# Loading and multiplying the first query projection chunk by chunk for all eight heads

## The chip, the cores and the metric

One core of one Trainium2 chip. The metric is the device time of one execution in microseconds, as a median over runs. The profiles are each of one execution; a profile's span is some 1.8 us shorter than the time of its run.

## The reference

Two independent attention blocks, A and B, whose outputs are concatenated. Each has its own x, cached K and V, and weights, all in bf16:

```python
B, Sq, D = 16, 32, 1024
Hq, Hkv, Sk, Dh = 32, 4, 512, 128
q = (x @ wq).reshape(B, Sq, Hq, Dh).transpose(0, 2, 1, 3)
scores = jnp.einsum("bhqd,bhkd->bhqk", q, k) * (Dh ** -0.5)
p = softmax(scores)
o = jnp.einsum("bhqk,bhkd->bhqd", p, v)
out = o.transpose(0, 2, 1, 3).reshape(B, Sq, Hq * Dh) @ wo
# ... the same for B; the two are concatenated on the last axis
```

What matters is the very first product: x @ wq for the first eight of A's 32 query heads. Nothing else can start before it. The sum over D = 1024 runs in eight chunks of 128.

## The kernel before

The start of the program loads x and the first eight heads' weights, multiplies them as they arrive, and only then enters the long loop over scores, values and projections. `load_w0(d0, d1, h0, h1, eng)` loads chunks d0 to d1 of the weights for heads h0 to h1, on SP's queue unless another engine is named. `load_x_transposed` loads two chunks of x through a transposing load. NF is 6, REP is 8, HC is 4, DC is 8, TT is 4.

```python
load_x(TT // 2, TT, nc.scalar)
# ...
load_x(0, TT // 2)
load_w0(0, 1, 0, NF // 2)              # chunk 0, heads 0..2   96 KB  SP
load_w0(0, 1, NF // 2, NF, nc.scalar)  # chunk 0, heads 3..5   96 KB  ACT
load_w0(1, 2, 0, NF)                   # chunk 1, heads 0..5  192 KB  SP
load_w0(2, 3, 0, NF, nc.scalar)        # chunk 2, heads 0..5  192 KB  ACT
load_x_transposed(2)
load_w0(3, 4, 0, NF)                   # chunk 3, heads 0..5  192 KB  SP
load_w0(0, HC, NF, REP)                # chunks 0..3, heads 6 and 7, rows of 512 bytes
load_w0(HC, HC + 1, 0, REP)            # chunk 4, all heads
# ... chunks 5 to 7 and the rest of x, then the loads of the main loop
warm_up(22)                            # matmuls on a constant, meant to raise the clock
for k, ts in enumerate(((0, TT // 2), (TT // 2, TT))):
    transpose_x(0, *ts, nc.vector.tensor_copy)
    transpose_x(1, *ts, nc.scalar.copy, spare[k])
for ts in ((0, TT // 2), (TT // 2, TT)):
    first_heads(range(0, NF // 2), (0,), *ts)   # chunk 0, heads 0..2, in two halves
first_heads(range(NF // 2, NF), (0,))           # chunk 0, heads 3..5
first_heads(range(NF), (1, 2, 3))               # chunks 1..3, heads 0..5
first_q += [...]                                # accumulators of heads 6 and 7
first_heads(range(NF, REP), range(HC))          # heads 6 and 7, chunks 0..3
first_heads(range(REP), range(HC, DC - 1))      # chunks 4..6, all heads
# ... chunk 7, then the copies out of PSUM; the main loop follows
```

Of the kernel before, what the change touches and what calls it, by code (L numbers as in the profile page):

```python
# [9 lines left out]
FP32 = mybir.dt.float32  # L10
# [6 lines left out]
P = 128  # L17
# [3 lines left out]
REP = HQ // HKV  # L21
# [160 lines left out]
def kernel(  # L182
# [14 lines left out]
    nc = tc.nc  # L197
# [3 lines left out]
    DC = D // P  # L201
# [3 lines left out]
    NW = 512  # L205
# [12 lines left out]
    def fast_path(ok_i):  # L218
        with ExitStack() as fctx:
# [6 lines left out]
            psum = enter(tc.tile_pool(name="psum", bufs=2, space=bass.MemoryType.PSUM))  # L226
# [190 lines left out]
            ob = {}  # L417
# [37 lines left out]
            NF = REP - 2  # L455
            HC = DC // 2
# [10 lines left out]
            def load_x_transposed(d0):  # L467
                nc.sync.dma_start_transpose(
                    out=xT[0][:, d0:d0 + 2, :],
                    in_=A_x.flatten_outer_dims()[:, d0 * P:(d0 + 2) * P],  # L470
                )

            def load_w0(d0, d1, h0, h1, eng=nc.sync):
                eng.dma_start(  # L474
                    out=w0[d0 // HC][:, d0 % HC:(d1 - 1) % HC + 1, h0 * DH:h1 * DH],
                    in_=wq_v[:, d0:d1, h0 * DH:h1 * DH],
                )
# [2 lines left out]
            nc.scalar.preload_act_table_set("natural_log_exp_and_others")  # L480
            load_x(0, TT // 2)
            load_w0(0, 1, 0, NF // 2)
            load_w0(0, 1, NF // 2, NF, nc.scalar)
            load_w0(1, 2, 0, NF)
            load_w0(2, 3, 0, NF, nc.scalar)
            load_x_transposed(2)
            load_w0(3, 4, 0, NF)
            load_w0(0, HC, NF, REP)
            load_w0(HC, HC + 1, 0, REP)
            load_x_transposed(HC)  # L490
            load_w0(HC + 1, DC - 1, 0, REP)
            load_x_transposed(HC + 2)
            load_w0(DC - 1, DC, 0, REP)
            load_wq(0, 2, 0, 2)
# [9 lines left out]
            first_q = []  # L504
# [12 lines left out]
            def transpose_x(d, t0, t1, copy, ps=None):  # L517
                if ps is None:
                    ps = psum.tile([P, NTOK], BF16, name="xT_ps", tag="ob")
                for tt in range(t0, t1):  # L520
                    nc.tensor.transpose(
                        ps[:, tt * P:(tt + 1) * P], x_sb[:, tt, d * P:(d + 1) * P], ident[:]
                    )
                ts = slice(t0 * P, t1 * P)
                copy(out=xT[0][:, d, ts], in_=ps[:, ts])

            def first_heads(heads, dcs, t0=0, t1=TT):
                ts = slice(t0 * P, t1 * P)
                for dc in dcs:
                    for h in heads:  # L530
                        nc.tensor.matmul(  # L531
                            first_q[h][:, ts],
                            lhsT=w0[dc // HC][:, dc % HC, h * DH:(h + 1) * DH],
                            rhs=xT[0][:, dc, ts],
                            start=(dc == 0 and t0 == 0),
                            stop=(dc == DC - 1),
                        )

            warm_up(22)
            for k, ts in enumerate(((0, TT // 2), (TT // 2, TT))):  # L540
                transpose_x(0, *ts, nc.vector.tensor_copy)
                transpose_x(1, *ts, nc.scalar.copy, spare[k])
            for ts in ((0, TT // 2), (TT // 2, TT)):
                first_heads(range(0, NF // 2), (0,), *ts)
            first_heads(range(NF // 2, NF), (0,))
            first_heads(range(NF), (1, 2, 3))
            first_q += [psum.tile([P, NW], FP32, name="q_ps", tag="ob")[:] for _ in range(2)]
            first_heads(range(NF, REP), range(HC))
            first_heads(range(REP), range(HC, DC - 1))
            for n, h in enumerate((0, 2, 4, 6, 5, 7, 1, 3)):  # L550
                first_heads((h,), (DC - 1,))
                copy = nc.vector.tensor_copy if n % 2 else nc.scalar.copy
# [115 lines left out]
    ok_i = flag.tile([1, 1], I32, name="ok_i")  # L668
    total = 2 * 2 * NG * QW
    ok = fast_path(ok_i)  # L670
    with tc.If(ok < total, preferred_fallthrough_block=True, label="general"):
        general_path(tc, problems, out_flat)
# [30 lines left out]
```

## Time and profile before

| | before |
|---|---|
| time, median of 3 runs | 343.0 us (342.91 to 343.46) |
| span of the profiled run | 341.1 us |
| TensorE busy | 98% of the span |
| chunk 1 lands / chunk 1's matmuls start | 6.23 / 6.28 us |
| first projection ends | 18.97 us |

The prediction below shows the chain and the waits. To these belongs the list of DMA issues from the start of the program (stretch 1.2 to 2.0 us). Its columns: tiles, the queue that issued, how often, size, and the time from issue to landing.

```profile
w_sb<-in_A_wq_dram SPq DMA_DIRECT2D x1, 192.0 KB, 4.5
w_sb<-in_A_wq_dram ACTq DMA_DIRECT2D x1, 192.0 KB, 4.7
x_sb<-in_A_x_dram ACTq DMA_DIRECT2D x1, 128.0 KB, 3.0
w_sb<-in_A_wq_dram SPq DMA_DIRECT2D x1, 96.0 KB, 2.8
w_sb<-in_A_wq_dram ACTq DMA_DIRECT2D x1, 96.0 KB, 3.0
```

The first two lines are chunk 1 (SP) and chunk 2 (ACT).

### The profile page before, as it was taken

What the parts mean: (1) busy time and instruction counts of PE and PEld (TensorE: products, weight loads), DVE (VectorE), ACT (ScalarE), POOL (GpSimd) and SP (SyncE); (2) the same over time, 40 slices, a digit from 0 to 9 for tenths busy, and PEclk for the clock granted to TensorE, in tenths of its full rate; (3) what the DMA queues carried; (4) which work ended last, traced back from release to release, by engine and by line L of the source; (5) the groups of instructions that cost most, each with busy time, mean ns of one, the idle gap of its engine ahead of it and who ended that gap; (6) DMA issues with size and microseconds to landing.
All of it is one profiled execution on the core that took longest, in us unless ns stands there. A gap on an engine that the chain in (4) does not pass through costs nothing.

```text
span 341.1 us, 5436 instructions
## 1 busy us (share of the span) xinstructions
PE 334.5 (98%) x2074; PEld 212.8 (62%) x2113; DVE 265.4 (78%) x335; ACT 185.3 (54%) x208; POOL 47.0 (14%) x206
## 2 busy tenths in 40 slices
PE   8999999999999999999999999999999999999996
PEld 5455666666666666666666666666666666666555
DVE  0047988888988898888888988879888888889540
ACT  2057666666667667666645545555554555555110
POOL 0001110011111111110012221222122101111100
PEclk9999999999999999999999999999999999999999
DMA  7999999999996998899999955998449995430001
GB/s 199 298 188 274 288 250 225 205 254 250 301 258 144 241 222 232 197 294 308 322 293 290 240 125 147 338 284 222 118 106 307 357 194 152 115 93 9 17 19 33
DMA packets 128622, 71.70 MB, mean 210 GB/s; under 512 B 76880, under 2 KB 127824, under 8 KB 128592
## 3 DMA queue, kind: packets, MB, share of 16 engines
q1 hardware_dynamic: 127504, 69.78, 82.5%
q0 software_dynamic: 384, 1.05, 0.8%
q10 hardware_dynamic: 704, 0.49, 0.5%
q8 instruction: 17, 0.28, 0.3%
q14 instruction: 13, 0.11, 0.1%
HBM read 50.59 MB, written 2.10 MB: 154 GB/s over the span
## 4 chain that ended last, share of the span: by engine, by line
PE 96%; DMA 2%; issue 1%; ACT 0%; SPq 0%; ACTq 0%
PE f_ps L320 31%; PE q_ps L301 28%; PE ob L425 17%; PE s_ps L357 16%; PE q_ps L531 4%; DMA w_sb<-in_A_wq_dram 1%; DMA out_dram<-o_sb 0%; ACT o_sb L329 0%; SPq L465 0%; SPq L474 0%; ACTq L329 0%; ACT p_sb L365 0%; ACTq L365 0%
## 5 line engine op out<-in xcount | busy, mean ns | idle before, releaser
L365 ACT ACTIVATE p_sb<-s_ps,shift 128x1024 bf16<-128x1024 f32 x128 | 142.7, 1115 | 97.5 <-PE s_ps L357 86.3
L376 DVE TRANSPOSE_TENSOR_REDUCE parts<-p_sb 128x32 f32<-128x1024 bf16 x128 | 158.7, 1240 | 20.8 <-ACT p_sb L365 19.3
L320 PE MATMUL f_ps<-wo_sb,oT 128*128 128x512 bf16 (+1 forms) x524 | 127.6, 366 | 0.6
L301 PE MATMUL q_ps<-xT,wq_sb 128*128 128x512 bf16 x430 | 113.0, 379 | 0.6
L425 PE MATMUL ob<-p_sb,v_sb 128*128 128x256 bf16 x512 | 76.8, 273 | 0.8
L357 PE MATMUL s_ps<-qT,kT 128*128 128x256 bf16 x512 | 76.8, 273 | 0.0
L320 PEld LDWEIGHTS <-oT 128*128 128x128 bf16 x544 | 53.2, 98 | 35.3
L357 PEld LDWEIGHTS <-kT 128*128 128x128 bf16 x512 | 56.9, 113 | 28.3
L301 PEld LDWEIGHTS <-wq_sb 128*128 128x128 bf16 x448 | 43.8, 98 | 32.2
L425 PEld LDWEIGHTS <-v_sb 128*128 128x128 bf16 x512 | 50.1, 98 | 20.0
L447 DVE TENSOR_TENSOR oT<-r,ob 128x512 bf16<-128x512 f32 x64 | 43.9, 686 | 19.8 <-PE ob L425 19.4
L411 DVE STREAM_TRANSPOSE r<-rall 128x512 f32<-128x512 f32 x64 | 44.2, 691 | 1.1
L309 ACT CAST qT<-q_ps 128x512 bf16<-128x512 f32 x56 | 32.7, 583 | 16.5 <-PE q_ps L301 16.5
L394 POOL COPY half<-cs 64x32 f32<-64x32 f32 x32 | 6.6, 206 | 231.5 <-DVE cs L384 231.4
L329 ACT CAST o_sb<-f_ps 128x512 bf16<-128x512 f32 (+1 forms) x17 | 9.5, 559 | 23.6 <-PE f_ps L320 23.6
L531 PE MATMUL q_ps<-xT,w_sb 128*128 128x512 bf16 (+1 forms) x66 | 14.1, 369 | 0.6 <-DMA w_sb<-in_A_wq_dram 0.6
L406 DVE RECIPROCAL rall<-sums 128x32 f32<-128x32 f32 x32 | 10.4, 326 | 3.3 <-POOL sums L403 3.3
L384 DVE TENSOR_REDUCE cs<-parts 128x32 f32<-128x128 f32 x32 | 12.1, 377 | 1.1
L553 DVE CAST qT<-q_ps 128x512 bf16<-128x512 f32 x4 | 2.5, 683 | 13.2 <-PE q_ps L531 13.2
L531 PEld LDWEIGHTS <-w_sb 128*128 128x128 bf16 x67 | 6.4, 97 | 8.0 <-DMA w_sb<-in_A_wq_dram 1.1
L553 ACT CAST qT<-q_ps 128x512 bf16<-128x512 f32 x4 | 2.1, 599 | 12.8 <-PE q_ps L531 12.8
L331 POOL DMA_DIRECT2D out_dram<-o_sb x8 | 4.6, 575 | 29.2 <-ACT o_sb L329 29.2
(25 smaller groups left out, 48.1 us busy)
## 6 DMA issues: line engine op xcount, KB each, us to landing
v_sb<-in_A_v_cache_dram SPq DMA_DIRECT2D x16, 512.0 KB, 5.4
wq_sb<-in_B_wq_dram SPq DMA_DIRECT2D x8, 1024.0 KB, 6.0
wo_sb<-in_A_wo_dram SPq DMA_DIRECT2D x8, 1024.0 KB, 7.5
v_sb<-in_B_v_cache_dram SPq DMA_DIRECT2D x16, 512.0 KB, 4.6
wo_sb<-in_B_wo_dram SPq DMA_DIRECT2D x8, 1024.0 KB, 8.5
wq_sb<-in_A_wq_dram SPq DMA_DIRECT2D x5, 1024.0 KB, 6.7
wq_sb<-in_A_wq_dram SPq DMA_DIRECT2D x2, 512.0 KB, 7.3
kT<-in_A_k_cache_dram SPq DMA_TRANSPOSE x64, 4.4
```

Source lines behind the costliest of these rows:

```text
L301: nc.tensor.matmul(ps[:], lhsT=w[:, dc, (h % 4) * DH:(h % 4 + 1) * DH], rhs=xT[pr][:, dc, :], start=(dc == 0), stop=(dc == DC - 1),)
L309: nc.scalar.copy(out=qT[pr, g][:, :, hl, :], in_=ps[:].rearrange("p (b s) -> p b s", s=SQ),)
L320: nc.tensor.matmul(ps[:, 0:width], lhsT=oT[pr, tt][:, h, :], rhs=wo_tiles[pr, nh, h // REP][:, h % REP, off:off + width], start=(h == 0), ...
L357: nc.tensor.matmul(s_ps[:, c, :], lhsT=kT[:, i % GRP, c, :], rhs=qT[pr, g][:, b, :, :].rearrange("p h s -> p (h s)"), start=True, stop=True,)
L365: nc.scalar.activation(out=p_sb[:], in_=s_ps[:], func=ACTF.Exp, bias=shift[:], scale=SCALE)
L376: nc.vector.tensor_reduce(out=parts[k][:, q, :, :].rearrange("p c h -> p (c h)"), in_=st[i]["p"][:].rearrange("p c (h s) -> p (c h) s", s=SQ),
L384: nc.vector.tensor_reduce(out=cs[:], in_=parts.pop(k)[:].rearrange("p q c h -> p q h c"), axis=AX.X, op=ALU.add,)
L406: nc.vector.reciprocal(out=rall[:, k, :], in_=quad.pop(k)[:])
L411: nc.vector.transpose(out=r[:].rearrange("p n s -> p (n s)"), in_=rall[:, k, o * 2 * REP:(o + 1) * 2 * REP] .unsqueeze(2).to_broadcast([P, ...
L425: nc.tensor.matmul(ob[j][:, q, :], lhsT=v_sb[:, i % GRP, c, :], rhs=st[i]["p"][:, c, :], start=(c == 0), stop=(c == KC - 1),)
L447: nc.vector.tensor_tensor(out=out, in0=rcp.pop(j)[:].rearrange("p (q h) s -> p q h s", h=REP), in1=ob.pop(j)[:].rearrange("p q (h s) -> p ...
L531: nc.tensor.matmul(first_q[h][:, ts], lhsT=w0[dc // HC][:, dc % HC, h * DH:(h + 1) * DH], rhs=xT[0][:, dc, ts], start=(dc == 0 and t0 == 0 ...
```

## The change

The intent: load each chunk in one piece for all eight heads, in rows of 2 KB, alternating between the two queues at first. Heads 6 and 7 then join from chunk 0 on instead of following after chunk 3, and the 512-byte rows go.

```diff
-            load_w0(0, 1, NF // 2, NF, nc.scalar)
-            load_w0(1, 2, 0, NF)
-            load_w0(2, 3, 0, NF, nc.scalar)
+            load_w0(0, 1, NF // 2, REP, nc.scalar)
+            load_w0(1, 2, 0, REP)
+            load_w0(2, 3, 0, REP, nc.scalar)
             load_x_transposed(2)
-            load_w0(3, 4, 0, NF)
-            load_w0(0, HC, NF, REP)
+            load_w0(3, 4, 0, REP)
             load_w0(HC, HC + 1, 0, REP)
             load_x_transposed(HC)
-            load_w0(HC + 1, DC - 1, 0, REP)
+            for d in range(HC + 1, DC - 1):
+                load_w0(d, d + 1, 0, REP)
@@
+            first_q += [psum.tile([P, NW], FP32, name="q_ps", tag="ob")[:] for _ in range(2)]
             for ts in ((0, TT // 2), (TT // 2, TT)):
                 first_heads(range(0, NF // 2), (0,), *ts)
-            first_heads(range(NF // 2, NF), (0,))
-            first_heads(range(NF), (1, 2, 3))
-            first_q += [psum.tile([P, NW], FP32, name="q_ps", tag="ob")[:] for _ in range(2)]
-            first_heads(range(NF, REP), range(HC))
-            first_heads(range(REP), range(HC, DC - 1))
+            first_heads(range(NF // 2, REP), (0,))
+            first_heads(range(REP), range(1, DC - 1))
```

## The prediction

> **What bounds the kernel now.** I read the page from the top: busy shares, then the slices, then the chain of work that ended last, and from there only the first 24 us, because the change touches nothing later.
>
> The page's busy line, slices and chain:
>
> ```profile
> span 341.1 us, 5436 instructions
> ...
> PE 334.5 (98%) x2074; PEld 212.8 (62%) x2113; DVE 265.4 (78%) x335; ACT 185.3 (54%) x208; POOL 47.0 (14%) x206
> ...
> PE   8999999999999999999999999999999999999996
> ...
> PEclk9999999999999999999999999999999999999999
> ...
> PE 96%; DMA 2%; issue 1%; ACT 0%; SPq 0%; ACTq 0%
> ```
>
> TensorE is busy in every slice at the full granted clock, and 96% of the chain is matmuls. A matmul that is saved, or a wait that is added, anywhere on it moves the end by its own length. DMA has 2% of the chain, which is where the change acts. The chain in order of time over the first 24 us (start, length, what) shows it:
>
> ```profile
> 1.26 0.44 SPq L474
> 1.70 0.05 issue
> 1.75 4.48 DMA w_sb<-in_A_wq_dram
> 6.23 0.05 issue
> 6.28 2.33 PE q_ps L531 x10
> 8.61 0.05 issue
> 8.66 10.31 PE q_ps L531 x47
> 18.97 0.43 PE q_ps L301 x2
> ```
>
> The end of the program hangs on one load: the second load that SP issues for w_sb, which is chunk 1 of the weights (six heads, 192 KB). It is issued at about 1.7 us, lands at 6.23, and from 6.28 TensorE runs without a wait: 57 recorded matmuls (58 in the program, one record is missing) until 18.97, then straight into the rest. So 12.69 us for 58, or 0.2188 us each. The waits of TensorE, asked over the whole program, are only two:
>
> ```profile
> PE q_ps L513 <- PEq L687: 0.9, 1, 0.9
> PE q_ps L531 <- DMA w_sb<-in_A_wq_dram: 0.6, 1, 0.6
> ```
>
> The first is the program's start. The second is the wait that this change can move: TensorE has finished chunk 0 and sits 0.6 us until chunk 1 lands. The same spot in the timeline of TensorE (start, length, group):
>
> ```profile
> 3.40 0.88 PE L521 MATMUL xT_ps<-ident,x_sb 128*128 128x128 bf16 x8
> 4.17 1.50 PE L531 MATMUL q_ps<-xT,w_sb 128*128 128x256 bf16 x9
> 6.28 12.69 PE L531 MATMUL q_ps<-xT,w_sb 128*128 128x512 bf16 x57 [0.59 <-DMA w_sb<-in_A_wq_dram]
> ```
>
> The nine matmuls from 4.17 to 5.67 are chunk 0: three heads in two halves each, then three whole ones. How fast the loads go while this wait is set, and later when only 2-KB rows move, the DMA view tells (stretches 3.2 to 6.3 and 10.45 to 11.6 us):
>
> ```profile
> DMA packets 1201, 0.72 MB, mean 232 GB/s; under 512 B 747, under 2 KB 1201, under 8 KB 1201
> q1 hardware_dynamic: 906, 0.42, 71.7%
> q10 hardware_dynamic: 295, 0.30, 31.9%
> ...
> DMA packets 290, 0.39 MB, mean 339 GB/s; under 512 B 112, under 2 KB 112, under 8 KB 290
> ```
>
> In the first stretch both queues (q1 is SP's, q10 ACT's) share the engines, rows are 768 or 1,536 bytes, and pieces of 256 bytes of a transpose come in: 232 GB/s. In the second, SP alone moves 2-KB rows: 339 GB/s.
>
> **What the Trainium skill says.** "DMA: Bandwidth & Descriptors", section "Queues, rings and completion order": each DMA engine takes turns between the queues it has work for, a packet at a time. The trace agrees: both queues have data in the same stretch (0.42 and 0.30 MB). So bytes that are added to ACT's queue delay SP's chunk 1 too. The same page, section "Issuing engines are not separate DMA queues", says that loads from several engines run on the same 16 DMA engines and interleave; so the two queues are no second source of bandwidth. "Perfetto Trace Analysis", section "DMA Optimizations", says that transfers under 2 KB carry a significant overhead each; 339 against 232 GB/s is in line with it, although the slower stretch also holds the transpose, so rows are not its only difference. "TensorE: Matmul & The Clock Gate", part 1, says that the clock halves after an idle window of about 3.4 us; the trace has 0.59 us of idle here and the granted clock stays 1.00, so it doesn't contradict it.
>
> **The change part by part.** The count and shape of matmuls stay the same: 67 in this stage (6 halves and 61 whole). Bytes stay the same: 2 MB of weights, 1 MB of x apart from the 256 KB read twice. SP issues ten loads of this stage after its x in both kernels, ACT two.
>
> 1. Moved to before the wait: heads 6 and 7 of chunk 0. Chunk 0 becomes 6 halves and 5 whole matmuls, and 56 instead of 58 come after the wait: 2 x 0.2188 = 0.44 us less after it. Before the wait, chunk 0 ends at 5.67 + 0.44 = 6.11 instead of 5.67. That alone would eat most of the 0.59 us of idle time, for free: a gain of 0.44 us if chunk 1 landed when it does now.
>
> 2. But chunk 1 lands later. Its load grows from 192 to 256 KB, and the part of chunk 0 on ACT's queue, which shares the engines with it, from 96 to 160 KB. SP's own part of chunk 0 (96 KB) and the x loads are as before; chunk 2's extra 64 KB on ACT's queue lies mostly behind. So 128 KB more pass before chunk 1 is complete. At 232 GB/s that is 131,072 B / 232 = 0.56 us; at the 339 of 2-KB rows 0.39 us. I take 0.48. The wait then ends at 6.28 + 0.48 = 6.76 (between 6.67 and 6.84).
>
> 3. The part on ACT's queue: now "96 KB, 3.0 us" from issue at 1.34, so it lands at 4.34. With 64 KB more, at half of 232 GB/s as the queues share, up to 0.56 us later, 4.9. Head 3 needs it at 4.17 + 6 half matmuls of 0.11 = 4.83. A stall of 0.1 us is possible, but chunk 0 then ends at 6.2, still before 6.76: it costs nothing.
>
> 4. Later chunks. Chunk 2 needs its weights and its transposed x at 6.76 + 8 x 0.2188 = 8.51. The transpose is issued at 2.22 and takes 5.2 us now, so 7.42; 192 KB more lie ahead of it or beside it (64 each in chunk 0, 1 and 2): 0.58 to 0.85 us, so 8.0 to 8.3. It holds, by 0.2 to 0.5 us; this is the narrow place. Chunk 3 (192 KB now lands at 3.7 + 4.5 = 8.2) has 256 KB more before its end, so about 9.2, and is needed at 10.26. Chunk 4 has the same bytes ahead of it as now, with the 512-byte rows of heads 6 and 7 gone, lands at 9.8 or earlier and is needed at 12.0. Everything after lands as now or a little earlier and has 1 us or more of slack.
>
> 5. After 18.97 nothing changes: the same instructions in the same order on every engine, and TensorE has no wait left there that an earlier load could shorten.
>
> Sum: +0.48 us for the later landing, -0.44 us for two matmuls that go before it, so +0.04 us (between -0.05 and +0.12). On 343.0 that is 343.0 to 343.1. **I predict 343.1 us.** The gain in load efficiency of the 2-KB rows comes in a stage in which, after chunk 1, TensorE is the slower side.
>
> **Rivals.**
> - Chunk 1 lands hardly later (about 6.4), because 2-KB rows move faster and the 256-byte transpose pieces start later and disturb less. For it: 339 against 232 GB/s. Against: on-chip queues share a packet at a time, so ACT's extra bytes still count. It would make 342.7.
> - The slowest DMA engine sets the landing. The mean rate says chunk 1 should be in by about 5.5, yet it lands at 6.23: some engines run well behind the others. If their lag grows with the bytes (192 to 256 KB, so 4/3 of the roughly 2.3 us that it now takes to move), the wait ends at about 7.0: 343.3.
> - The wait moves on to chunk 2, if the transposed x lands after its slack of 0.2 to 0.5 us: 0.2 to 0.5 us more, 343.3 to 343.6. The slow transpose pieces speak for it; against it, whatever delays the transpose delays chunk 1 as well, and both slide together.
> - The longer idle time lowers the clock: with under 1 us of idle time the trace gives no reason, and it would make about 344.7 if half of a window of 3.4 us were lost.
>
> **Range and chances.** The worked-out spread of the wait's end, 6.4 to 7.3, gives -0.3 to +0.6 us; runs of the kernel before spread from 342.91 to 343.46. So 342.5 to 343.8 for eight in ten. Two per cent is 6.9 us; the whole stage before the first wait's end is 6.3 us and cannot be lost or gained by this. Faster by over 2%: 0.005; within 2%: 0.985; slower by over 2%: 0.01.
>
> **What would show it.** In the chain, the load of chunk 1 should end at 6.7 to 6.8 and be followed by matmuls of this stage until 18.9 to 19.1, without a second wait; in the timeline of TensorE, eleven matmuls of chunk 0 from about 4.2 and then an idle piece of 0.5 to 0.8 us; the granted clock stays 1.00. I am wrong in step 2 if chunk 1 lands before 6.5 or after 7.1; in step 4 if a second DMA wait shows at chunk 2 or 3; in step 5 if the stage ends within 0.2 us of 18.97 but the program's time moves by more than that.

## The result, and the profile after

| | before | changed |
|---|---|---|
| time, median of 6 runs each | 343.42 us (342.91 to 343.6) | 343.72 us (342.86 to 344.47) |
| mean of the same runs | 343.30 us | 343.68 us |
| span of the profiled run | 341.1 us | 341.9 us |
| chunk 1 lands / its matmuls start | 6.23 / 6.28 us | 7.46 / 7.50 us |
| first projection ends | 18.97 us | 19.76 us |
| last group of matmuls starts | 324.84 us | 325.64 us |

The ratio is 1.0011, 95% interval 0.9993 to 1.0029: the same within 2%, and inside the predicted range. Ratios throughout are the mean time of one kernel's fast runs over that of the other's fast runs of the same rounds, so not quite the ratio of the medians.

The chain of work of the changed kernel over the first 24 us (start, length, what):

```profile
1.25 0.44 SPq L474
1.70 0.05 issue
1.75 5.71 DMA w_sb<-in_A_wq_dram
7.46 0.05 issue
7.50 2.12 PE q_ps L531 x9
9.62 0.05 issue
9.67 10.09 PE q_ps L531 x46
19.76 0.65 PE q_ps L301 x3
```

The shape is the predicted one: one wait for chunk 1, then matmuls without a break. But chunk 1 is in flight for 5.71 us instead of 4.48. TensorE's timeline (start, length, group):

```profile
4.20 2.44 PE L531 MATMUL q_ps<-xT,w_sb 128*128 128x256 bf16 x11
7.50 12.26 PE L531 MATMUL q_ps<-xT,w_sb 128*128 128x512 bf16 x55 [0.86 <-DMA w_sb<-in_A_wq_dram]
```

Chunk 0 has its eleven matmuls and ends at 6.64, not at the forecast 6.11; then comes 0.86 us of idle time. After it there are 12.26 us of matmuls instead of 12.69. The issues of the first loads, as above for the kernel before:

```profile
w_sb<-in_A_wq_dram SPq DMA_DIRECT2D x1, 256.0 KB, 5.7
w_sb<-in_A_wq_dram ACTq DMA_DIRECT2D x1, 256.0 KB, 5.9
w_sb<-in_A_wq_dram ACTq DMA_DIRECT2D x1, 160.0 KB, 4.0
```

Chunks 1 and 2 again land together, both 1.2 us later than before. The span differs by 0.8 us: 1.22 us of later start less 0.43 us of matmuls, and both ends of the program repeat it (19.76 against 18.97, 325.64 against 324.84). So the accounting closes in this pair of profiles, and what is open is why chunk 1 came so late, and whether one pair of profiles can be trusted when runs of one kernel differ by 0.7 to 1.6 us.

My theory: chunk 2 on ACT's queue, which takes turns with chunk 1, holds it up by more than I had counted. Rivals: the profile caught a bad run; or some engines are slow in this part of the program whatever the queues do.

### The profile page after: what moved, and what is told of

Its sections match the earlier page's. It is cut to its first block, busy times and chain, and to the rows that moved or that the text cites. A ratio compares the mean times of both kernels' runs of the same rounds, so it can differ in the third digit from the quotient of the medians.

```text
span 341.9 us, 5436 instructions
## 1 busy us (share of the span) xinstructions
PE 335.0 (98%) x2074; PEld 213.1 (62%) x2113; DVE 265.1 (78%) x335; ACT 185.2 (54%) x208; POOL 46.7 (14%) x206
## 4 chain that ended last, share of the span: by engine, by line
PE 95%; DMA 2%; issue 1%; ACT 0%; SPq 0%; ACTq 0%
PE f_ps L320 31%; PE q_ps L301 28%; PE ob L425 17%; PE s_ps L357 16%; PE q_ps L531 4%; DMA w_sb<-in_A_wq_dram 2%; DMA out_dram<-o_sb 0%; ACT o_sb L329 0%; SPq L465 0%; SPq L474 0%; ACTq L329 0%; ACT p_sb L365 0%; ACTq L365 0%
```

## The experiments

All kernels gave correct results. "Before" below is the median of the kernel before in the same call, 9 or 10 runs.

### The changed kernel again (after_again)

No edit.

> The changed kernel, unaltered, once more with five rounds, to separate what belongs to the change from what belongs to one profiled run. In the two profiles so far the span is the landing of chunk 1 plus a constant: 341.13 - 6.28 = 334.85 us after the wait in the kernel before, 341.9 - 7.50 = 334.4 us in the changed one. Theory (the later landing is real): the wait ends at 7.0 to 8.0 us again, the span is again 334.4 us more than that, and the mean time is 0.2 to 0.6 us above before (ratio 1.0006 to 1.0018). Rival (the profile caught a bad run and the working of the prediction holds): the wait ends at 6.6 to 6.9 and the ratio is within 1.0004.

Measured: 343.51 us, before 343.38, ratio 1.0004 (0.9991 to 1.0018). The wait ended even later, at 7.71. The chain of this run:

```profile
1.75 5.91 DMA w_sb<-in_A_wq_dram
7.66 0.05 issue
7.71 2.12 PE q_ps L531 x9
```

The span, 342.1, is again 334.4 more than 7.71. The late landing was not one bad run, though this profile fell on the slowest of the five. The mean of the five times, 343.56, is 0.24 us above before's 343.32, less than the profiles alone suggest; the ratio fell below the range that I had given for the theory and is what I had written for the rival. So at this point the later landing was shown but its whole effect on the time was not.

### The loads alone (loads_only)

```diff
-            first_q += [...]            # ahead of chunk 0
@@
-            first_heads(range(NF // 2, REP), (0,))
-            first_heads(range(REP), range(1, DC - 1))
+            first_heads(range(NF // 2, NF), (0,))
+            first_heads(range(NF), (1, 2, 3))
+            first_q += [...]            # as in the kernel before
+            first_heads(range(NF, REP), range(HC))
+            first_heads(range(REP), range(HC, DC - 1))
```

> The loads of the changed kernel with the matmul order of the kernel before (chunk 0 for six heads, chunks 1 to 3 for six heads, then heads 6 and 7 of chunks 0 to 3). It takes away the half of the change that should gain. Theory (two parts: a later landing, and two matmuls moved before it, worth 2 x 0.219 us): the wait ends where the changed kernel has it, about 7.5, 58 matmuls follow it, and the time is 0.44 us above the changed kernel, about 0.8 above before (ratio 1.0018 to 1.003). Rival (the order of matmuls is worth nothing, for instance since the six heads have their data no later): the time is that of the changed kernel within 0.15 us.

Measured: 344.03 us, ratio to before 1.0025 (1.0011 to 1.0038). Its mean, 344.01, is 0.45 us above the mean of the changed kernel in the same rounds (343.56). That is what step 1 of the prediction gave for the two matmuls that the change moves ahead of the wait, 0.44 us; but the two sets of five overlap (343.42 to 344.55 and 343.1 to 344.0), so the times alone would not settle it. The profile fell on the fastest of the five runs. Its chain:

```profile
1.75 5.01 DMA w_sb<-in_A_wq_dram
6.76 0.05 issue
6.80 2.33 PE q_ps L531 x10
```

With exactly the loads of the changed kernel, chunk 1 landed at 6.76 in this execution, against 7.46 and 7.66, and the wait ended at 6.80, not at the theory's 7.5. So the landing itself varies by up to 0.9 us from run to run, and a single profile of each kernel cannot size it.

### Chunk 0 as before, chunks 1 to 3 whole (chunk0_in_parts)

```diff
-            load_w0(0, 1, NF // 2, REP, nc.scalar)
+            load_w0(0, 1, NF // 2, NF, nc.scalar)
             load_w0(3, 4, 0, REP)
+            load_w0(0, 1, NF, REP)
@@
-                        start=(dc == 0 and t0 == 0),
+                        start=(dc == (1 if h >= NF else 0) and t0 == 0),
@@
-            first_heads(range(NF // 2, REP), (0,))
-            first_heads(range(REP), range(1, DC - 1))
+            first_heads(range(NF // 2, NF), (0,))
+            first_heads(range(REP), (1, 2, 3))
+            first_heads(range(NF, REP), (0,))
+            first_heads(range(REP), range(HC, DC - 1))
```

> The changed kernel, but chunk 0 loaded and multiplied as before: 96 KB of it on ACT's queue, heads 6 and 7 of it loaded after chunk 3 and multiplied after chunk 3. Chunks 1 to 3 stay whole. 64 KB fewer than in the changed kernel lie ahead of chunk 1, 64 KB more than before. Theory (each 64 KB ahead of or in chunk 1 costs about 0.4 us, as 1.2 us for 128 KB in the two profiles, or 0.8 us by the means of the times, say): chunk 1 lands at 6.6 to 7.1, midway, and 58 matmuls follow it, so the time is between before + 0.2 and before + 0.8 us, equal to or up to 0.3 us above the changed kernel. Rival (2-KB rows of chunk 1 alone make it late, the bytes on ACT's queue don't count): it lands at 7.2 to 7.6, time before + 0.9 us or more. Second rival (ACT's 160 KB alone make it late): it lands at 6.2 to 6.4, time as before.

Measured: 344.37 us, ratio 1.0028 (1.0014 to 1.0041), 1.0 us above before by the medians. Chunk 1 landed at 7.19. The 64 KB fewer in ACT's first load brought nothing that the runs show. That is the outcome that I had written for the rival, that the bytes on ACT's queue don't count. But there is another reading: with a shorter first load, ACT's queue reaches chunk 2 sooner, and chunk 1 shares with that instead. The issues say for this run 5.4 us for chunk 1 and 5.6 for chunk 2, together as always.

### Chunk 2 behind chunk 1 on SP's queue (chunk2_on_sp)

```diff
-            load_w0(2, 3, 0, REP, nc.scalar)
+            load_w0(2, 3, 0, REP)
```

> The changed kernel with one word taken away: chunk 2's load is issued on SP's queue behind chunk 1 instead of on ACT's queue beside it. The same bytes in the same rows. Theory (chunk 1 lands late because the packets of ACT's queue take turns with it on the same engines): chunk 1 lands at 5.3 to 6.2 instead of 7.46, the wait for it nearly goes (chunk 0 ends at about 6.1 to 6.6), chunk 2 and the transposed x still land before they are needed, and the time is 0.8 to 1.4 us below the changed kernel and 0.4 to 1.0 us below before (ratio about 0.998). Rival (a few engines are slow in this part of the program whatever the queues): chunk 1 lands at 7.0 or later again, ratio 1.000 to 1.002. Second rival (the wait moves): chunk 1 lands early but chunk 2 or its transposed x is waited for, and the time is within 0.3 us of before.

Measured: 342.53 us, ratio to before 0.9986 (0.9973 to 1.0000). The two readings are told apart here. From this kernel's issues (same columns; stretch 1.6 to 2.2 us), chunk 1 and the two parts of chunk 0:

```profile
w_sb<-in_A_wq_dram SPq DMA_DIRECT2D x1, 256.0 KB, 3.9
w_sb<-in_A_wq_dram ACTq DMA_DIRECT2D x1, 160.0 KB, 3.7
w_sb<-in_A_wq_dram SPq DMA_DIRECT2D x1, 96.0 KB, 2.7
```

Chunk 1 lands 3.9 us after its issue at 1.70, at about 5.6, with the same 256 KB in the same 2-KB rows and the same part of chunk 0 on ACT's queue. Besides chunk 2 itself, the transposing load behind it moved: SP issues it at 2.69 instead of 2.22 us. In the two runs below that issue chunk 2 late on ACT's queue it stays at 2.22, and there chunk 1 landed 4.3 and 4.5 us after its issue, against 3.9 here and 5.0 to 5.9 with chunk 2 beside it. So most of the gain belongs to chunk 2, and 0.2 to 0.6 us of it may belong to the transposing load. Chunk 2 itself, issued at 2.2, lands 4.5 us later at 6.7, a whole microsecond before it did on ACT's queue in the changed kernel (issued at 1.8, 5.9), though in loads_only it landed there at 6.9. TensorE no longer waits for chunk 1. Its chain now begins with the other early load, ACT's part of chunk 0, and after it no load is waited for:

```profile
1.34 3.69 DMA w_sb<-in_A_wq_dram
5.03 0.05 issue
5.08 3.20 PE q_ps L531 x14
8.28 0.05 issue
8.33 10.09 PE q_ps L531 x46
```

This is the clearest difference in time of the whole set: the mean, 342.75, is 0.81 us below that of the changed kernel in the same rounds (343.56), while a difference of two such sets of five is uncertain by about 0.2 us (standard error, worked out from the runs).

I first put the late landing down to the rate as well: that two large loads at once run slower than one behind the other. The rate in the stretch from 3.2 to 5.6 us, in the changed kernel and then in this one (packets, bytes, rate, and packets under a size), seems to say so:

```profile
DMA packets 324, 0.49 MB, mean 205 GB/s; under 512 B 29, under 2 KB 162, under 8 KB 324
```

```profile
DMA packets 473, 0.65 MB, mean 270 GB/s; under 512 B 94, under 2 KB 253, under 8 KB 473
```

Other runs refute it. The same stretch of loads_only, and of chunk3_on_act_too below, both with chunk 2 on ACT's queue beside chunk 1:

```profile
DMA packets 604, 0.75 MB, mean 311 GB/s; under 512 B 79, under 2 KB 379, under 8 KB 604
```

```profile
DMA packets 519, 0.67 MB, mean 281 GB/s; under 512 B 81, under 2 KB 310, under 8 KB 519
```

At 281 GB/s chunk 1 still landed at 7.38, and here at 270 GB/s at 5.6. What tells these two apart is not how much moved but whose bytes: of the 0.67 MB there SP's queue had 0.33, of the 0.65 MB here 0.49.

### The same again (chunk2_on_sp_again)

No edit beyond the last one.

> The changed kernel with chunk 2 on SP's queue, once more, since its first five runs fell into two groups (three at 342.5, two at 343.1 and 343.3). No load is waited for in it, so what is left to vary is the clock of TensorE at the start: in the profiles the matmuls of chunk 0 and 1 run at half speed (0.43 us for a whole one) until some point between 4.0 and 6.7 us. Theory (the clock's release sets the time where no load does): again 342.4 to 343.3, mean ratio 0.998 to 0.999, and in the profile the break-free matmuls end at 18.4 if the release is at about 4, and later by half of the delay of the release. Rival (the first set was luck): the mean is within 0.0005 of before.

Measured: 342.94 us, before 343.25, ratio 0.9995 (0.9982 to 1.0009): in the range of times that I had named, but the ratio's mean missed the range 0.998 to 0.999. Chunk 1 landed 4.1 us after issue, the rate in the same stretch was 321 GB/s, and there was again no wait for chunk 1. The first projection ended at 18.69 instead of 18.42. Over both sets of five, this kernel's mean is 342.89 us, against 343.29 for the kernel before, 0.4 us or 0.12% less. It is the best of all versions tried, by an amount that the second set alone does not separate from nothing.

### The same edit in the kernel before (before_chunk2_on_sp)

```diff
-            load_w0(2, 3, 0, NF, nc.scalar)
+            load_w0(2, 3, 0, NF)
```

> The kernel before with the one word taken away that helped the changed one: chunk 2's load on SP's queue behind chunk 1. Theory (the turn-taking of the two queues makes chunk 1 late in this kernel too): chunk 1 lands by about 5.2 to 5.6, the wait goes or nearly goes, TensorE runs without a break from about 4.1 until the end of the stage at 18.4 to 18.8, time 342.4 to 342.8 (ratio 0.997 to 0.9985). With no wait left the two orders of matmuls are worth the same, so it equals the changed kernel with that edit within 0.2 us. Rival (the whole rows are needed too: 1.5-KB rows and the 512-byte rows of heads 6 and 7 leave a wait for chunk 2 or its transposed x): 343.0 or more.

Measured: 342.99 us, before 343.34, ratio 0.9989 (0.9975 to 1.0002). Chunk 1 lands 3.8 us after issue instead of 4.5, at about 5.5, and no wait of the matmuls for a load is listed; the rate from 3.2 to 5.6 us is 259 GB/s, against 251 in the kernel before. So the landing is the theory's, but the time missed its 342.4 to 342.8, and the stage ended at 19.04, not by 18.8. The rival's wait is not there either; what held the stage up is the speed of the first matmuls, told of in the next section. The edit brings chunk 1 in earlier in both kernels, and with it the two orders of matmuls differ little (means 342.93 here, 342.75 and 343.03 in the changed kernel). What both had in common was chunk 2's load on the second queue.

### The kernel before again (before_again, before_third)

No edit; two more profiles, one of them with five rounds.

> The kernel before, unaltered, for a second profile of it and to see what five rounds make of no difference. The first profile, from which the prediction worked (wait ends at 6.28), fell on one of the shortest runs (342.92; its runs spread to 343.6). If the last matmul always follows the end of the wait by the same time, a typical run of it should end its wait at about 6.6 to 6.9. Theory (the profile that the prediction was worked from was a lucky one): the wait ends at 6.4 to 7.0 in a run of 343.1 to 343.6. Rival: it ends at 6.2 to 6.35 whatever the run's time. The ratio should be 1.000 within 0.0007.

> A third profile of the kernel before, unaltered, for the landing of its chunk 1. Theory (the landing of chunk 1 in it is 6.2 to 6.5, and the rest of the spread between its runs is the clock): it lands at 6.1 to 6.6; if chunk 0's matmuls are at half speed they end at about 6.7 and there is no wait. Rival: it lands as late as in the changed kernel (7 or later) in some runs.

Measured: before_again 343.39 us, before 343.34, ratio 1.0004 (0.9991 to 1.0018), which is what no difference looks like in five rounds. In before_third (one run, 343.39 us) chunk 1 landed at 6.71, just outside the 6.1 to 6.6 of its theory and short of its rival's 7. In before_again it landed 4.7 us after its issue, at about 6.4, and yet the matmuls show no wait for it. The reason is in the matmuls of this line. First the kernel before, then before_again (count, and shortest, median and longest in ns):

```profile
L531 PE MATMUL q_ps<-xT,w_sb x66: 269/379/390, 4.2 to 18.6; 128*128 128x512 bf16 x60, 128*128 128x256 bf16 x6
```

```profile
L531 PE MATMUL q_ps<-xT,w_sb x66: 379/379/634, 4.1 to 19.0; 128*128 128x512 bf16 x60, 128*128 128x256 bf16 x6
```

The longest takes 634 ns instead of 390. The stretches 5.30 to 6.60 and 9.30 to 10.60 us of before_again, for this line alone (stretch, length, TensorE busy and matmuls that touch it, weight loads, granted clock, DMA share, GB/s):

```profile
5.30:6.60 1.30, 1.30 (x5) 0.42 (x4) 1.00 1.21 253
9.30:10.60 1.30, 1.30 (x8) 0.59 (x7) 1.00 1.31 139
```

In the same 1.30 us only five matmuls are under way instead of eight; the starts in the trace are 0.43 us apart there and 0.22 later. So in this execution the matmuls of chunk 0 ran at half speed and ended at about 6.7, later than chunk 1 landed. The clock column says 1.00 for both stretches, because the trace has no record of the clock before 6.64 us and the view prints 1.00 where there is none. In each of the 14 profiles the first record, of full clock, begins somewhere between 3.95 us (the first profile of the kernel before) and 6.64 us (before_again), and in these two the matmuls change their spacing at that very moment, at 4.00 and 6.66 us. So the column could not show how long the first matmuls run at half speed, and that time varies from execution to execution. In the profile that the prediction was worked from, chunk 0 took 1.50 us at full speed. It was a favourable execution in two ways: full speed from the start of chunk 0, and chunk 1 at 6.23, the earliest of three.

### Chunks 1 and 2 in halves on both queues (halves_on_both)

```diff
-            load_w0(1, 2, 0, REP)
-            load_w0(2, 3, 0, REP, nc.scalar)
+            load_w0(1, 2, 0, HC)
+            load_w0(1, 2, HC, REP, nc.scalar)
+            load_w0(2, 3, 0, HC)
+            load_w0(2, 3, HC, REP, nc.scalar)
```

> The changed kernel with chunks 1 and 2 each cut into heads 0 to 3 on SP's queue and heads 4 to 7 on ACT's, in rows of 1 KB: two queues are at work at the same time as in the changed kernel, with the same bytes, but now both work on chunk 1 first. Theory (what hurts is that half of the engines' turns go to chunk 2 while chunk 1 is awaited): the first half of chunk 1 lands at 4.9 to 5.7, the wait is gone or under 0.2 us, time 342.4 to 342.9. Rival (two queues at once are slow in themselves, as is seen in packets that take 0.3 to 1.2 us): chunk 1 still lands at 6.5 or later and the time is within 0.3 us of before or above it.

Measured: 343.59 us, before 343.34, ratio 1.0007 (0.9994 to 1.0019). My theory failed here: SP's half of chunk 1 landed 4.8 us after its issue at about 1.75, so at about 6.5, not at 4.9 to 5.7. Putting chunk 1 first on both queues does not bring it in early. The time and the landing are those that I wrote for the rival, that two queues with large loads at once are slow in themselves; but the rate from 3.2 to 5.6 us was 249 GB/s, and loads_only had 311 with two queues, so the rival's reason is not shown. Two more things weaken it as evidence: the matmuls of chunk 0 ran at half speed in this profile too, so TensorE waited for weights only 0.2 us, and the rows are 1 KB.

### Chunk 2 late on ACT's queue (chunk2_late_on_act, chunk2_late_act_mended)

First try: the same load, issued after ACT's two copies of transposed x.

```diff
-            load_w0(2, 3, 0, REP, nc.scalar)
@@
                 transpose_x(1, *ts, nc.scalar.copy, spare[k])
+            load_w0(2, 3, 0, REP, nc.scalar)
```

> The changed kernel with chunk 2's load still on ACT's queue and whole, but issued after ACT's two copies of transposed x, at about 4.7 instead of 1.8 us. Its data then starts at about 6.7 (1.8 to 2.0 us after the issue), when chunk 1 is in. Theory (when chunk 2 moves matters, not whose queue it is on): chunk 1 lands at 5.2 to 5.8 and its wait goes; chunk 2 lands at about 7.5 to 8.2 and is needed at about 7.9, so either no wait or one of up to 0.4 us: time 342.4 to 343.0. Rival (a load on ACT's queue beside SP's is what is slow): chunk 2 lands at 8.5 or later and the time is 343.4 or more.

Measured: 350.93 us, ratio 1.0210 (1.0191 to 1.0229). Neither theory is tested, because the edit made a wait of its own:

```profile
3.94 4.60 DMA w_sb<-in_A_wq_dram
8.54 0.02 issue
8.56 6.27 DMA w_sb<-in_A_wq_dram
14.83 0.05 issue
14.88 0.61 PE q_ps L530
```

The built program gives its loads eight completion semaphores in turn (numbers 100 and 103 to 109 in the trace), and a load that gets one still in use waits for it. ACT's load got the one of chunk 3, issued at 3.94 on SP and landed at 8.54; it was issued at 8.56, and TensorE sat 6.3 us.

Second try: all loads after chunk 1 are emitted after the transposes in the program text, so that the semaphore is a free one.

> The late issue of chunk 2 on ACT's queue again, mended. In the first try ACT's load had been given a completion semaphore that chunk 3's load still held, so it was not issued before 8.56. Now the loads after chunk 1 are emitted after the transposes in the program, and the load waits for a semaphore that the first x load has long released. It should be issued at about 4.7, and its data start at 6.3 to 6.8. Theory (when chunk 2 moves matters, not on which queue): chunk 1 lands at 5.3 to 6.0, nearly as with chunk 2 on SP's queue (5.65), chunk 2 at 7.3 to 8.2; time 342.4 to 343.1, below before. Rival (ACT's queue is slow beside SP's): chunk 2 lands after 8.5, time 343.5 or more.

Measured: 345.20 us, before 343.25, ratio 1.0060 (1.0040 to 1.0080). Now the load was issued at 4.54, as intended, and chunk 1 landed at about 6.0, as the theory said (in the first try at about 6.2): without chunk 2 beside it, chunk 1 is early also when chunk 2 stays on ACT's queue. But chunk 2 needed 5.61 us from its issue, and landed at 10.15; TensorE waited 2.10 us:

```profile
4.54 5.61 DMA w_sb<-in_A_wq_dram
10.15 0.05 issue
```

In the DMA view of the stretch 4.6 to 7.0 us only SP's queue has moved anything:

```profile
DMA packets 1142, 0.51 MB, mean 211 GB/s; under 512 B 1018, under 2 KB 1018, under 8 KB 1142
## 3 DMA queue, kind: packets, MB, share of 16 engines
q1 hardware_dynamic: 1142, 0.51, 113.1%
```

ACT's queue (q10) got its first packet more than 2.4 us after the issue. For chunk 2 the rival's numbers came out: this load on ACT's queue, beside a busy SP queue, was slow to start and slow to land. Why it starts so late is left open.

The idle time also showed what a longer wait does. Stretches of this run, for the same matmul line (columns as above):

```profile
10.20:11.40 1.20, 1.15 (x5) 0.54 (x7) 0.92 1.06 327
11.40:14.40 3.00, 3.00 (x9) 1.07 (x8) 0.50 1.14 324
14.40:17.40 3.00, 3.00 (x15) 1.38 (x14) 0.96 1.32 287
```

After 2.10 us of idle time and 1.2 us of work, the granted clock is 0.50 for 3 us. By the mean clocks of the runs this happened in two of the six (0.995, at 346.45 and 346.78 us); in the other four the mean stayed at 1.000 (344.57 to 345.46 us).

### Chunk 3 on ACT's queue too (chunk3_on_act_too)

```diff
             load_w0(2, 3, 0, REP, nc.scalar)
+            load_w0(3, 4, 0, REP, nc.scalar)
             load_x_transposed(2)
-            load_w0(3, 4, 0, REP)
```

> The changed kernel with chunk 3's load taken from SP's queue and put on ACT's, behind chunk 2. In every profile so far with chunk 2 on ACT's queue, chunks 1 and 2 landed within 0.4 us of each other (4.5 and 4.7 us after issue before, 5.7 and 5.9 in the changed kernel, 5.0 and 5.1 with its loads alone), though the queues take turns. Theory A (chunk 1 lands when all that is on ACT's queue at that time is in too, so all of the added bytes count and not only those ahead of it): with 256 KB more on ACT's queue chunk 1 lands later, at 8 us or more, time 344.2 or more. Theory B (turns by row: only as many of ACT's bytes count as SP has itself, and chunk 3's come after): chunk 1 lands at 6.7 to 7.7 as in the changed kernel, time 343.3 to 344.1.

Measured: 343.67 us, before 343.25, ratio 1.0015 (1.0001 to 1.0028). Chunk 1 landed 5.6 us after issue and chunk 2 5.7, as in the changed kernel; 256 KB more behind them on ACT's queue made no difference. Theory A is out, and theory B's numbers came: chunk 1 is held up by the one large load beside it, not by everything that is queued.

## Why the prediction was right or wrong

**The time.** 343.1 us forecast, 343.72 measured as a median (a later set: 343.51), inside 342.5 to 343.8; "within 2%" was right. The forecast difference was +0.04 us; the means differ by 0.38 us in the first set and 0.24 in the second, neither clear of noise. The range was wide enough to hold the time although step 2 failed, so the hit says little for the working: by the prediction's own sign, a landing after 7.1, step 2 was wrong.

**Step 1, two matmuls ahead of the wait: right.** 0.44 us forecast; 0.43 in the chains (12.69 against 12.26 us); the 0.45 between the means with and without that part agrees, but is not clear of noise.

**Step 2, the later landing of chunk 1: right in direction, mis-sized.** Forecast +0.48 us, to 6.67 to 6.84. The kernel before landed it at 6.23, about 6.4 and 6.71 in three profiles, mean 6.45; the changed kernel's loads at 7.46, 7.66 and 6.76, mean 7.29. That is +0.84 us from three profiles each, and with step 1 gives 0.84 - 0.44 = +0.40, near the 0.38 and 0.24 measured as times. It is a rough figure: the two groups all but touch (6.71 and 6.76), and in before_again the half-speed matmuls, not the landing, set the pace. The term of the step that failed is the bytes that pass before chunk 1 is complete:
- "chunk 2's extra 64 KB on ACT's queue lies mostly behind". It does not. In every profile with chunk 2 issued on ACT's queue beside chunk 1, the two land within 0.4 us of each other, and with chunk 2 moved behind chunk 1 on SP's queue chunk 1 lands 1 to 2 us earlier. Counting that part too, 192 KB are added and not 128; at the forecast's own 232 GB/s that is 0.85 us, an estimate that meets the 0.84. It is no proof: chunk0_in_parts, with 64 KB fewer of them, landed at 7.19 all the same.

That the rate of 232 to 339 GB/s failed is not shown: with large loads on both queues it was 205 to 311 GB/s from run to run.

My base was also off: the one profile before had the earliest landing of three and matmuls at full speed. Three smaller readings were wrong, with little weight in the sum: no part of x is read twice (its first two chunks are loaded plain and the other six only transposed); the stretch at 339 GB/s is not of 2-KB rows alone, since 112 of its 290 packets are under 512 B; and the passage on small transfers that the prediction names speaks of whole transfers under 2 KB, not of rows within a load of 192 KB.

**Step 3, ACT's part of chunk 0: right that it costs nothing, wrong in size.** It landed 4.0 us after its issue, at 5.3 rather than at 4.9 or before, and chunk 0 ended at 6.64 rather than 6.2, still before chunk 1. Part of that was clock: the first matmuls ran at half speed until 5.20, which I did not expect because the clock column said 1.00.

**Steps 4 and 5: right in outcome.** No second wait came; chunk 2 landed at 7.7 and its x at 8.5 (issued at 2.22, 6.3 us), later than the forecast 8.0 to 8.3, but chunk 2 was needed only at 9.25, since all had slid with chunk 1. Everything later was carried through: the last group of matmuls starts 0.80 us later, as the first projection ends 0.79 us later.

**The rivals.** The second, a lag that grows with the bytes and a wait that ends at about 7.0, came nearest, and the traces bear out part of its mechanism. In the packet records each load ends with sixteen packets of 4 bytes (one for each DMA engine, to judge by their number), and chunk 1 counts as landed 0.4 to 0.6 us after the last of them. In the changed kernel chunk 1's sixteen come between 4.63 and 7.05 us; in chunk3_on_act_too fifteen are in by 5.42 and the last comes at 6.82. With chunk 2 issued late (chunk2_late_act_mended) they come between 4.43 and 5.59. So the last part does set the landing, and chunk 2 beside it makes the last part late; which engine lags, and why, is not shown. The clock did not fall in the 0.86 us of idle time, as forecast; it did after 2.10 us.

**What stays open.** Why the parts of chunk 1 end up to 2.4 us apart when chunk 2 moves beside it, and why a late load on ACT's queue takes over 2.4 us to move its first packet: the traces show that they do, not the cause. Halving the chunks across both queues did not settle it. And whether the change itself costs time is not shown: over both sets the means differ by 0.31 us, with a standard error of 0.16.

## What to carry to other kernels

Where one load holds up the start, put the next large load behind it on the same queue: beside it on a second queue, it made the first land 0.7 to 2 us later in these two kernels. Take the moving of work ahead of a wait and the landing of the load as two separate terms, and size the second from several profiles; in a single execution it varied by up to 0.9 us for identical loads. Before trusting a busy figure in the first microseconds, look at the spacing of the matmuls, not only at the clock column, which may have no record yet.

## What the Trainium skill lacked or had wrong

- "DMA: Bandwidth & Descriptors", section "Issuing engines are not separate DMA queues", says that issuing on several engines saves only the time of the sequencer. Here it cost: chunk 1 landed 5.0 to 5.9 us after issue with chunk 2 on ACT's queue, 3.9 and 4.1 with chunk 2 behind it on SP's.
- The same page, section "Latency and other measured facts", puts the first byte of a load issued from SP or ACT at about 0.6 us. A load on ACT's queue issued at 4.54 us beside a busy SP queue had moved nothing by 7.0.
- "TensorE: Matmul & The Clock Gate", part 1, names an idle window of about 3.4 us before the clock is halved. After an idle time of 2.10 us, and 1.2 us of work, the granted clock was 0.50 for 3 us, in two of six runs of that kernel.
- That TensorE starts at half speed is stated in the same part of that page; I had not used it. What no page says is that a profile's clock column can read 1.00 meanwhile (five matmuls in 1.30 us where eight fit later), since the first clock record begins only at 3.95 to 6.64 us.
